# A planner that counts TensorE's switches of tiling, a regular beat for the agents' stage, and a later load of w_out

## The chip, the core and the metric

The kernel runs on one core of a Trainium2 chip. The core has five engines with queues of their own: TensorE (PE; its weight loads are shown as PEld), VectorE (DVE), ScalarE (ACT), GpSimd (POOL) and SyncE (SP), which here issues every DMA. The metric is the device time of one execution in microseconds. The time before is the median of three runs, 1548.81 us (1548.41 to 1549.6).

## The reference

```python
def _attn_ref(q, k, v, agents):            # q, k, v: (4, 12608, 128); agents: (4, 49, 128)
    def sm(a, b): softmax over the last axis of scale * a @ b.T
    agent_v = sm(agents, k) @ v            # (4, 49, 128)
    return sm(q, agents) @ agent_v         # (4, 12608, 128)

def _moe_ref(x, w_in, w_out, g_ln):        # x: (50432, 128), d_ff 1024
    h = x @ w_in
    e = np.exp(h - h.max(-1)); sm = e / (e.sum(-1) + 1e-09)
    solu = h * sm
    ln = (solu - mean(solu)) / sqrt(var(solu) + 1e-06) * g_ln
    return ln @ w_out
```

The second function takes the first one's output, flattened over the four batches. `w_in` and `w_out` arrive as 64-bit floats and are turned into 32-bit floats on the chip.

## The kernel before

**Three stages.** The *agents' stage* (`phase_a`, one call for each batch) goes through the 12608 keys in 13 chunks of 1024 (the last one shorter). For a chunk c it makes the logits of the 49 agents, padded to 64, against the keys (`p1_mm`, line 418, called step M1 here), takes a running maximum (L423, L430) and the exponentials (L444), transposes them on TensorE (L451, step TT), copies them out of PSUM (L457, step ET, on ACT or DVE as the planner likes), and multiplies with v (`p2_mm`, L467, step M2). After the last chunk some small steps (g1 to g7, f0 to f4) make a matrix for the batch, agent_v times w_in, in a high and a low part (`mh`, `ml`). The *q stage* (`phase_b`) works on units of eight tiles of 128 rows of q: logits against the agents (`b0`, L647, step B0), softmax, transposes (L682), and a DMA that lays out the weights pT. The *c stage*, the bulk, goes tile by tile (x = 0 to 395): h in PSUM (`c_h`, L747), maximum (L751), exponential (L761), u (L766), squares (L772), transposes (`c_t`, L779), evictions and a split into high and low parts (L794 to L811), the product with w_out (`c_w`, L827, 24 matmuls for two tiles), and the scaling by the standard deviation.

**Column tiling.** M1, M2 and B0 have stationary operands with 64 columns. Two such matmuls stand side by side in the array, one for PSUM partitions 0 to 63 and one for 64 to 127. Every other step uses all 128 columns. The planner has a mark for that, `kind`: 2 for M1, M2 and B0, 0 for `c_h` and `c_w`, 1 for the rest. A row of adjacent kind-2 steps is called a segment here.

**The order is written out ahead.** Each step is an `op` with an engine, a cost in microseconds, a due time in units of tiles, and what it depends on. `Plan.run` plays the kernel through with these costs: of each engine's candidates it takes those that can start within EPS of the earliest (0.01 us for PE) and of these the one with the lowest due time; of the engines it takes the one that starts first. The instructions come out in that order, and a chain of dependencies (L1029 to L1036) fixes it for each engine except SP, whose order is that of its issues. The costs and due times thus change nothing but the order. SWITCH adds a cost when PE goes from one kind to another: before, nothing into kind 2, and 0.087 or 0.033 us out of it.

**Shared room.** There are four PSUM banks (`px`) for everything but h; an op with `take` waits for a free one, and `free` gives it back: M1 holds its bank until L444 has read it, B0 until L659, the transposes until they are evicted, and one bank holds the sums of `c_w` for four tiles. The chunks of k and v have two buffers each in batches two to four; in batch one, where nothing else runs yet, eight chunks of each fit into buffers of the later stages.

**The head.** For the first batch SP issues (dues near -199) k chunk 0, both halves of w_in, and then k and v chunks in turn, the first q unit after chunk 7, w_out behind v chunk 7 (`VA = 7`), and the second q unit behind v chunk 12 (`VA1 = 12`). The conversions from 64 bits (`pair_f64`, L263) run on DVE, ACT and POOL. That of w_in (`cin`, due -100 + CPR) is needed by step f3 (L531), that of w_out (`cout`) by the first exponential of the c stage, whose buffers it borrows, and what follows it on POOL (L308 to L327), ACT (L331) and DVE (L334) by the first `c_w`.

Of the kernel before, what the change touches and what calls it, by code (L numbers as in the profile page):

```python
# [14 lines left out]
ALU = mybir.AluOpType  # L15
# [10 lines left out]
class Plan:  # L26
# [3 lines left out]
           "AA": 0.0, "AG": 0.17, "GP": 0.25, "GD": 0.1, "GG": 0.1, "GA": 0.2}  # L30
    EPS = {"P": 0.01, "A": 0, "D": 0.07, "G": 2.6, "S": 0.0}

    SWITCH = ((0.0, 0.0, 0.0), (0.0, 0.0, 0.0), (0.087, 0.033, 0.033))

    def __init__(self, banks):
        self.banks = [[0.0, b] for b in banks]
# [25 lines left out]
    def run(self, idle=None):  # L62
        while True:
            best = None
            for e, ops in self.cand.items():
                if not ops:
                    continue
                free = [b[0] for b in self.banks if b[0] is not None]
                first = min(free) if free else None
                at, opts, low = self.at[e], [], None  # L70
                for o in ops:
                    s = max(at, o.ready[e])
                    if o.take:
                        if first is None:
                            continue
                        s = max(s, first)
                    opts.append((s, o))
                    low = s if low is None else min(low, s)
                if low is None:
                    continue  # L80
                s, o = min((z for z in opts if z[0] <= low + self.EPS[e]), key=lambda z: z[1].due)
                if o.shy > 0.0:
                    s, o = min((z for z in opts if z[0] <= s + o.shy), key=lambda z: z[1].due)
                if best is None or s < best[0]:
                    best = (s, e, o)
            if best is None:
                break
            s, e, o = best
            for z in o.eng:
                self.cand[z].remove(o)  # L90
            if o.take:
                can = [b for b in self.banks if b[0] is not None and b[0] <= s]
                bank = max(can, key=lambda b: b[0])
                bank[0], o.bank = None, bank
            if idle is not None and e == "P":
                idle(s - self.at[e])
            o.start, o.by = s, e
            if e == "S":
                hold, size, lag = o.cost
                self.at[e] = s + hold  # L100
                if size:
                    self.dma = max(self.dma, s + 2.0) + size / 0.36
                    o.end = self.dma + 0.3
                else:
                    o.end = s + lag
            else:
                c = o.cost[o.eng.index(e)] if len(o.eng) > 1 else o.cost
                if e == "P":
                    c += self.SWITCH[self.kind][o.kind]
                    self.kind = o.kind  # L110
                o.end = self.at[e] = s + c
            if o.free is not None:
                o.free.bank[0] = o.end + self.LAT[e + "P"]
            if o.fn:
                args = [o.bank[1]] if o.take else []
                if len(o.eng) > 1:
                    args.append(e)
                o.fn(*args)
            for z in o.outs:
                z.left -= 1  # L120
                if not z.left:
                    self.push(z)
# [3 lines left out]
def kernel(  # L126
# [15 lines left out]
    P = 128  # L142
# [4 lines left out]
    NCK = N // (CT * P)  # L147
    CKT = N - NCK * CT * P
    AP2 = 64
    ETE = "AD"  # L150
    CPR = -1.98
    UTB = 4
    DIR = {(1, 0), (1, 1), (3, 1), (5, 1), (7, 1)}
    LGC = 8
    UB = 8
    TD = 2
    WC = 4

    BD0 = 13.69
    BD1 = 8.27  # L160
    BD2 = 9.96
    BD3 = -18.57
    BD4 = 0.41
    BD5 = 5.85
    DH = -3.05
    DMX = -3.31
    DEX = 7.76
    DU_ = 6.48
    DSQ = 21.68
    DT = -0.42  # L170
    DEV = -6.42
    DLD = 1.96
    DSP = 2.68
    DW = 3.31
    DR = 2.33
    DF_ = 5.14
    OUTD = -5.86
    OUTC = -74.58
    VA = 7
    VA1 = 12  # L180
    QA = 8
    WA = 0.5
    VLAG = 0.25
    PTB = 8
    SHY = -2.99
    DHR = -4.59
    DHL = -5.42
    DMXR = 10.02
    DMXL = 15.46
    DEXR = 5.1  # L190
    DEXL = -1.93
    DUR = -10.64
    DUL = -12.84
    DSQR = -10.36
    DSQL = -12.17
    DTR = -6.53
    DTL = -23.81
    DEVR = -0.65
    DEVL = 9.51
    DLDR = -16.59  # L200
    DLDL = 26.96
    DSPR = -6.09
    DSPL = 14.43
    DWR = 0.63
    DWL = -0.21
    RBL = 6.0
    ASTART = -3.67
    AEND = -2.04
    engs = (mybir.EngineType.PE, mybir.EngineType.Activation, mybir.EngineType.DVE, mybir.EngineType.Pool)
    SCALE = 1.0 / math.sqrt(C)  # L210
    INV = 1.0 / DF
# [28 lines left out]
    SL, SR = ALU.logical_shift_left, ALU.logical_shift_right  # L240

    def pair_f64(dst, names):

        ts, tt, stt = nc.vector.tensor_scalar, nc.vector.tensor_tensor, nc.vector.scalar_tensor_tensor
        gt = nc.gpsimd.tensor_tensor
        z = {}

        def tmp():
            for k, tg in (("s", "e"), ("a", "e"), ("e", "u"), ("m", "u")):
                t = epool.tile([P, 2, HW], I32, tag=tg, bufs=2, name=f"c{k}_{names}")  # L250
                for h in range(2):
                    z[k, h] = t[:, h, :]
            for h in range(2):
                z["lo", h], z["hi", h] = (words[names, h][:, :, i] for i in range(2))
                z["r", h], z["d", h], z["di", h] = z["m", h].bitcast(F32), dst[h], dst[h].bitcast(I32)

        def op(k, f, out, cost, **ins):
            def go(h):
                if not z:
                    tmp()  # L260
                kw = {n: (z[v, h] if n != "in1" or f is not gt else z[v, h].bitcast(F32)) if isinstance(v, str) else v
                      for n, v in ins.items()}
                f(out=z[out, h], **kw)  # L263

            return [(k, lambda h=h: go(h), cost) for h in range(2)]

        ops = (
            op("D", ts, "m", 0.34, in0="lo", scalar1=3, scalar2=3, op0=SL, op1=SR)
            + op("A", nc.scalar.mul, "r", 0.52, in_="m", mul=2.0 ** -52)
            + op("D", ts, "e", 0.34, in0="hi", scalar1=1, scalar2=21, op0=SL, op1=SR)  # L270
            + op("D", ts, "e", 0.34, in0="e", scalar1=-896, scalar2=0, op0=ALU.add, op1=ALU.max)
            + op("D", ts, "e", 0.34, in0="e", scalar1=255, scalar2=None, op0=ALU.min)
            + op("D", ts, "s", 0.34, in0="e", scalar1=23, scalar2=None, op0=SL)
            + op("D", ts, "a", 0.34, in0="hi", scalar1=12, scalar2=9, op0=SL, op1=SR)
            + op("G", gt, "r", 1.23, in0="r", in1="s", op=ALU.mult)
            + op("D", tt, "a", 0.6, in0="s", in1="a", op=ALU.bitwise_or)
            + op("D", stt, "a", 0.6, in0="lo", scalar=29, in1="a", op0=SR, op1=ALU.bitwise_or)
            + op("G", gt, "d", 1.23, in0="r", in1="a", op=ALU.add)
            + op("D", stt, "di", 0.6, in0="hi", scalar=-(2 ** 31), in1="di", op0=ALU.bitwise_and, op1=ALU.bitwise_or)
        )  # L280
        return ops[::2], ops[1::2]

# [80 lines left out]
    op = plan.op  # L363
# [9 lines left out]
    def phase_a(b, due, gate):  # L373

        head = b == 0
# [170 lines left out]
        def st(f, *x):  # L546
            return lambda *y: f(*x, *y)
# [2 lines left out]
        sz = lambda c: 0.524 if c < NCK else 0.164  # L550
        fr = lambda c: 1.0 if c < NCK else 0.5
        total = NC * 2.55 + 5.0
        at = lambda z: due[0] + (due[1] - due[0]) * z / total
        bg = op("G", begin, 0.0, at(0), gate)
        K, M1, E1, N1, V, M2, EE, TT, ET, AC = ({} for _ in range(10))

# [12 lines left out]
        for c in range(NC):  # L569
            kop(c)  # L570
            if not head:
                kop(c + 1)
            z = c * 2.55
            M1[c] = op("P", st(p1_mm, c), (0.876 if c < NCK else 0.449) + (0.8 if head and c == 0 else 0.0), at(z),
                       [K[c], M1.get(c - 1), TT.get(c - 2)], take=True, kind=2)
            E1[c] = op("D", st(p1_max, c), 0.6, at(z + 0.3), [M1[c], bg])
            N1[c] = op("D", st(p1_nm, c), 0.07, at(z + 0.4), [E1[c], N1.get(c - 1)])
# [1 line left out]
            if c:  # L579
# [1 line left out]
            TT[c] = op("P", st(p2_t, c), 0.435 * fr(c), at(z + 1), [EE[c], M2.get(c - 2)], take=True)  # L581
            ET[c] = op(ETE, st(p2_et, c), (0.478 * fr(c), 0.6 * fr(c)), at(z + 1.2), [TT[c]], free=TT[c])
            vop(c)
            M2[c] = op("P", st(p2_mm, c), 1.043 if c < NCK else 0.485, at(z + 1.5),
                       [ET[c], V[c], M2.get(c - 1), AC.get(c - 2)], take=True, kind=2)
            AC[c] = op("D", st(p2_ev, c), 0.26, at(z + 1.8), [M2[c], FC.get(c), AC.get(c - 1)], free=M2[c])
        if head:
# [2 lines left out]
        z = NC * 2.55 - 1.5  # L590
# [10 lines left out]
        z = NC * 2.55 + 1.0  # L601
# [32 lines left out]
    def phase_b(k, dues, gate=()):  # L634
# [76 lines left out]
        prev, first = None, None  # L711
        for j0, j1 in chunks:
            f = (lambda px, j0=j0, j1=j1: b0(j0, j1, px)) if prev is None else (lambda j0=j0, j1=j1: b0(j0, j1))
            o = op("P", f, 0.155 * (j1 - j0), dues[0] + 0.1 * j0,
                   [BQ[k], prev, B0.get(k - 1)] + [B4.get((k - 2, q)) for q in range(2)] + list(gate), take=prev is None, kind=2, shy=shy)
            first = first or o
            prev = o
# [224 lines left out]
    def at(x, d, r, l):  # L942
        return x + d + (r * (1.0 - x / 12.0) if x < 12 else l if x >= (B - 1) * TB else 0.0)
# [134 lines left out]
```

## Time and profile before

| what | before |
|---|---|
| median of three runs | 1548.81 us (1548.41 to 1549.6) |
| profiled execution, its own time | 1548.65 us |
| span of its instructions | 1546.9 us |
| TensorE clock granted | 1.0 throughout |
| DVE, ACT, POOL busy | 89%, 92%, 81% of the span |

A timeline row gives the start, the time until the end of the last instruction in the row, the engine, the line, and what is written and read. A matmul's busy time includes its way through the array, so neighbours overlap: what a step takes from TensorE is read from start to start. "x16" is a count of instructions merged into a row. A value in square brackets is idle time before it, with what ended it.

### The profile page before, as it was taken

The numbers are of one execution on the slowest core, as the hardware profiler recorded it, in microseconds if no ns is written. First come the engines' busy times: TensorE is split into PE (matmuls) and PEld (weight loads), VectorE is DVE, ScalarE is ACT, GpSimd is POOL, SyncE is SP. The second block draws the span as 40 slices with busy tenths as digits, with TensorE's granted clock in tenths as the row PEclk, the third lists the DMA queues.
The fourth block names the chain that finished last, engine by engine and source line by source line (L and its number), as shares of the span: only waits on it lengthen the run. The fifth ranks groups of instructions, "written<-read, shape, count | busy, mean of one in ns | idle before, by whom it ended". The sixth has DMA issues, their size and how long they took to land.

```text
span 1546.9 us, 35512 instructions
## 1 busy us (share of the span) xinstructions
PE 1526.4 (99%) x12628; PEld 1356.1 (88%) x12628; DVE 1372.4 (89%) x2214; ACT 1421.6 (92%) x2738; POOL 1252.9 (81%) x1613
## 2 busy tenths in 40 slices
PE   8899999999999999999999999999999999999998
PEld 4588898998889889898898889898889999999998
DVE  6988998888898889898898889889899999999997
ACT  3599999999899999999999999999999999999997
POOL 1478878787888887888878887887788899898987
PEclk9999999999999999999999999999999999999999
DMA  9533333324233333332333334433222232222221
GB/s 370 186 104 100 107 98 115 117 69 127 81 97 118 103 110 117 112 102 83 106 98 101 111 97 117 116 100 105 78 76 75 68 90 76 71 82 70 68 62 46
DMA packets 114721, 159.65 MB, mean 103 GB/s; under 512 B 16240, under 2 KB 71152, under 8 KB 114544
## 3 DMA queue, kind: packets, MB, share of 16 engines
q1 hardware_dynamic: 114544, 157.39, 34.0%
q8 instruction: 100, 1.64, 0.4%
q14 instruction: 77, 0.63, 0.1%
HBM read 105.36 MB, written 26.02 MB: 85 GB/s over the span
## 4 chain that ended last, share of the span: by engine, by line
PE 95%; DVE 3%; ACT 1%; DMA 1%; issue 0%; SPq 0%; DVEq 0%; ACTq 0%
PE px L827 36%; PE ph L747 24%; PE px L779 23%; PE px L647 3%; PE px L467 3%; PE px L418 3%; PE px L451 1%; PE px L682 1%; PE px L531 0%; DMA pT<-pn 0%; DVE mxp L423 0%; DVE nm L751 0%; DMA kh<-in_kT_dram 0%; DVE ca_in L263 0%; DVE uL L803 0%
## 5 line engine op out<-in xcount | busy, mean ns | idle before, releaser
L811 POOL TENSOR_TENSOR uL<-uT,uH 128x1024 fp32r<-128x1024 f32 (+1 forms) x344 | 661.5, 1923 | 27.6
L751 DVE TENSOR_REDUCE nm<-ph 128x1 f32<-128x1024 f32 x396 | 481.3, 1217 | 50.5 <-PE ph L747 47.7
L766 DVE SCALAR_TENSOR_TENSOR u<-ph,e 128x1024 f32<-128x1024 f32 x396 | 479.0, 1217 | 34.6 <-ACT e L761 24.4
L772 ACT ACTIVATE sq<-u,su 128x1024 bf16<-128x1024 f32 x396 | 460.5, 1163 | 24.8 <-DVE u L766 20.4
L761 ACT ACTIVATE e<-ph,nm 128x1024 f32<-128x1024 f32 x396 | 445.9, 1128 | 31.9 <-DVE nm L751 30.7
L827 PE MATMUL px<-uL,wH 128*128 128x256 f32 x1584 | 466.9, 295 | 0.2 <-POOL uL L811 0.2
L827 PE MATMUL px<-uH,wH 128*128 128x256 f32 x1584 | 450.6, 284 | 1.8 <-DVE uL L803 1.8
L827 PE MATMUL px<-uH,wL 128*128 128x256 f32 x1584 | 448.1, 283 | 0.0
L779 PE MATMUL px<-ident,u 128*128 128x128 f32 x3168 | 425.5, 274 | 2.7 <-DVE uL L803 1.4
L779 PEld LDWEIGHTS px<-ident,u 128*128 128x128 f32 x3168 | 356.7, 141 | 55.2 <-issue 20.7
L807 POOL TENSOR_SCALAR uH<-uT 128x1024 fp32r<-128x1024 f32 (+1 forms) x344 | 298.3, 867 | 98.4 <-ACT uT L798 98.0
L747 PE MATMUL ph<-mh,pT 128*128 128x512 f32 x792 | 329.7, 416 | 1.6 <-DMA pT<-pn 1.3
L827 PEld LDWEIGHTS px<-uH,wH 128*128 128x128 f32 x1584 | 299.0, 189 | 16.9 <-issue 3.5
L747 PE MATMUL ph<-ml,pT 128*128 128x512 f32 x792 | 312.3, 394 | 0.0
L798 ACT COPY uT<-px 128x512 f32<-128x512 f32 x541 | 299.2, 589 | 11.9 <-PE px L779 3.0
L827 PEld LDWEIGHTS px<-uH,wL 128*128 128x128 f32 x1584 | 299.1, 189 | 8.6 <-issue 0.7
L827 PEld LDWEIGHTS px<-uL,wH 128*128 128x128 f32 x1584 | 298.9, 189 | 8.5 <-issue 4.6
L803 DVE TENSOR_TENSOR uL<-px,uH 128x512 fp32r<-128x512 f32 x251 | 168.8, 685 | 47.5 <-ACT uH L794 45.8
L747 PEld LDWEIGHTS ph<-mh,pT 128*128 128x128 f32 x792 | 149.3, 188 | 20.3 <-issue 3.4
L747 PEld LDWEIGHTS ph<-ml,pT 128*128 128x128 f32 x792 | 149.9, 189 | 17.7 <-issue 0.5
L794 ACT CAST uH<-px 128x512 fp32r<-128x512 f32 x251 | 143.7, 592 | 1.2 <-PE px L779 0.9
L846 POOL TENSOR_TENSOR y<-x,nhalf 128x4 f32<-128x4 f32 x99 | 100.1, 1011 | 7.7
(118 smaller groups left out, 1337.6 us busy)
## 6 DMA issues: line engine op xcount, KB each, us to landing
pT<-pn SPq DMA_DIRECT2D x392, 64.0 KB
rB<-dr SPq DMA_DIRECT2D x98, 256.0 KB
qt<-in_qT_dram SPq DMA_DIRECT2D x48, 512.0 KB
out_dram<-ob SPq DMA_DIRECT2D x95, 256.0 KB
kt<-in_kT_dram SPq DMA_DIRECT2D x36, 512.0 KB
vt<-in_v_dram SPq DMA_DIRECT2D x36, 512.0 KB
dr<-yr SPq DMA_DIRECT2D x392, 0.5 KB
kh<-in_kT_dram SPq DMA_DIRECT2D x12, 512.0 KB
```

The costliest lines, as they stand in the source:

```text
L747: nc.tensor.matmul(ph[:, sl], lhs, bmats[b]["mh" if m == 0 else "ml"][:, sl], start=(m == 0), stop=(m == 1))
L751: nc.vector.tensor_reduce(out=nms[x], in_=phs[x], op=ALU.max, axis=AX.X, negate=True)
L761: nc.scalar.activation(out=es[x], in_=phs[x], func=AF.Exp, bias=nms.pop(x), accum_out=st[G]["S"][:, j : j + 1])
L766: nc.vector.scalar_tensor_tensor(out=u, in0=phs[x], scalar=INV, in1=es[x], op0=ALU.mult, op1=ALU.mult, accum_out=su)
L772: nc.scalar.activation(out=sq, in_=u, func=AF.Square, bias=su, scale=-float(DF), accum_out=st[G]["Q"][:, j : j + 1])
L779: nc.tensor.transpose(pt[:, kf * P : (kf + 1) * P], us[x][0][:, k0 * P : (k0 + 1) * P], ident)
L794: nc.scalar.copy(out=uH, in_=pt)
L798: nc.scalar.copy(out=rr[x][:, hf * 4 : hf * 4 + 4, :], in_=pt)
L803: nc.vector.tensor_tensor(out=uL, in0=pt, in1=uH.bitcast(F32), op=ALU.subtract)
L807: nc.gpsimd.tensor_scalar(out=uH, in0=rr[x][:, k0:k1, :], scalar1=1.0, scalar2=0.0, op0=ALU.mult, op1=ALU.add)
L811: nc.gpsimd.tensor_tensor(out=uL, in0=rr[x][:, k0:k1, :], in1=uH.bitcast(F32), op=ALU.subtract)
L827: nc.tensor.matmul(po, wt[:, kf, :], ut[:, kf, :], start=(q == 0), stop=(q == WM - 1))
```

## The change

The planner gets a cost for going into kind 2 and a higher one for leaving it. While PE is in kind 2, any kind-2 op that can start within HOLD (0.17 us) of the earliest candidate is taken ahead of the others, whatever its due time. The planner's costs of M1, M2, B0 and of three conversion ops are set anew.

In batches two to four the agents' stage no longer spreads its steps over the time from ASTART to AEND, but goes at a fixed beat: a chunk each UB * ASP = 6.8 tiles (a q unit has 8). M2 of chunk c is due 6.8 * 2.36 / 2.55 = 6.3 tiles after its M1, so just ahead of the M1 of chunk c + 1 at 6.8; before it was due 1.5 / 2.55 of a beat of 7.0 tiles after its M1, which is 4.1.

In the head w_in is issued ahead of k chunk 0 (WA), v chunks come three k chunks later (VLAG), w_out moves behind k and v of chunk 12 (VA), and so stands ahead of the second q unit, which was there already. The first q unit's load has a later due time (QA). The conversion of w_in is due after the steps of the first batch's agents' stage instead of before them (CPR). The due times of the other steps have new values.

```diff
-    SWITCH = ((0.0, 0.0, 0.0), (0.0, 0.0, 0.0), (0.087, 0.033, 0.033))
+    SWITCH = ((0.0, 0.0, 0.12), (0.0, 0.0, 0.12), (0.18, 0.14, 0.0))
+
+    HOLD = 0.17
...
-                s, o = min((z for z in opts if z[0] <= low + self.EPS[e]), key=lambda z: z[1].due)
+                near = [z for z in opts if z[0] <= low + self.EPS[e]]
+                if e == "P" and self.kind == 2:
+                    near = [z for z in opts if z[0] <= low + self.HOLD and z[1].kind == 2] or near
+                s, o = min(near, key=lambda z: z[1].due)
...
-    CPR = -1.98
+    CPR = 1.32
...
-    BD0 = 13.69
-    BD1 = 8.27
-    BD2 = 9.96
-    BD3 = -18.57
-    BD4 = 0.41
-    BD5 = 5.85
-    DH = -3.05
-    DMX = -3.31
-    DEX = 7.76
-    DU_ = 6.48
-    DSQ = 21.68
+    BD0 = 14.77
+    BD1 = 12.82
+    BD2 = 19.94
+    BD3 = -16.84
+    BD4 = -1.74
+    BD5 = 4.61
+    DH = -3.24
+    DMX = 8.3
+    DEX = 0.49
+    DU_ = -2.17
+    DSQ = 18.46
...
-    OUTD = -5.86
+    OUTD = -13.17
...
-    VA = 7
+    VA = 12
...
-    QA = 8
-    WA = 0.5
-    VLAG = 0.25
+    QA = 22.85
+    WA = -5.59
+    VLAG = 0.61
...
-    ASTART = -3.67
-    AEND = -2.04
+    ASP = 0.85
+    MZ = 2.36
+    ASTART = -3.92
+    AEND = -6.25
...
-        at = lambda z: due[0] + (due[1] - due[0]) * z / total
+        at = lambda z: due[0] + (due[1] - due[0]) * z / total if head else due[0] + UB * ASP * z / 2.55
...
-            M1[c] = op("P", st(p1_mm, c), (0.876 if c < NCK else 0.449) + (0.8 if head and c == 0 else 0.0), at(z),
+            M1[c] = op("P", st(p1_mm, c), (0.95 if c < NCK else 0.51) + (0.8 if head and c == 0 else 0.0), at(z),
...
-            M2[c] = op("P", st(p2_mm, c), 1.043 if c < NCK else 0.485, at(z + 1.5),
+            M2[c] = op("P", st(p2_mm, c), 0.96 if c < NCK else 0.45, at(z + MZ) if not head else at(z + 1.5),
...
-            o = op("P", f, 0.155 * (j1 - j0), dues[0] + 0.1 * j0,
+            o = op("P", f, 0.128 * (j1 - j0), dues[0] + 0.1 * j0,
```

Left out are new values of the remaining due times and three costs of conversion ops (0.6 to 0.9).

More of the change, by code (lines that the diff above doesn't have):

```diff
@@ L157 @@
     WC = 4
-    BD0 = 13.69
-    BD1 = 8.27
-    BD2 = 9.96
-    BD3 = -18.57
-    BD4 = 0.41
-    BD5 = 5.85
-    DH = -3.05
-    DMX = -3.31
-    DEX = 7.76
-    DU_ = 6.48
-    DSQ = 21.68
-    DT = -0.42
[L171 to L176, printed above, removed]
-    OUTD = -5.86
+    BD0 = 14.77
[9 more added lines that the diff above has]
+    DSQ = 18.46
+    DT = -0.42
+    DEV = -7.32
+    DLD = 2.24
+    DSP = -1.16
+    DW = 3.3
+    DR = 15.18
+    DF_ = 5.63
+    OUTD = -13.17
     OUTC = -74.58
-    VA = 7
+    VA = 12
     VA1 = 12
-    QA = 8
-    WA = 0.5
-    VLAG = 0.25
+    QA = 22.85
+    WA = -5.59
+    VLAG = 0.61
     PTB = 8
[L185 to L192, printed above, removed]
+    SHY = -0.0
+    DHR = -4.39
+    DHL = -5.43
+    DMXR = -5.18
+    DMXL = 10.25
+    DEXR = 23.76
+    DEXL = -1.81
+    DUR = -10.37
     DUL = -12.84
-    DSQR = -10.36
+    DSQR = -10.73
     DSQL = -12.17
     DTR = -6.53
-    DTL = -23.81
-    DEVR = -0.65
+    DTL = -23.89
+    DEVR = -12.92
     DEVL = 9.51
@@ L202 @@
     DSPR = -6.09
-    DSPL = 14.43
-    DWR = 0.63
+    DSPL = 14.3
+    DWR = 2.02
     DWL = -0.21
     RBL = 6.0
-    ASTART = -3.67
-    AEND = -2.04
+    ASP = 0.85
+    MZ = 2.36
+    ASTART = -3.92
+    AEND = -6.25
     engs = (mybir.EngineType.PE, mybir.EngineType.Activation, mybir.EngineType.DVE, mybir.EngineType.Pool)
@@ L275, in pair_f64 @@
             + op("G", gt, "r", 1.23, in0="r", in1="s", op=ALU.mult)
-            + op("D", tt, "a", 0.6, in0="s", in1="a", op=ALU.bitwise_or)
-            + op("D", stt, "a", 0.6, in0="lo", scalar=29, in1="a", op0=SR, op1=ALU.bitwise_or)
+            + op("D", tt, "a", 0.9, in0="s", in1="a", op=ALU.bitwise_or)
+            + op("D", stt, "a", 0.9, in0="lo", scalar=29, in1="a", op0=SR, op1=ALU.bitwise_or)
             + op("G", gt, "d", 1.23, in0="r", in1="a", op=ALU.add)
-            + op("D", stt, "di", 0.6, in0="hi", scalar=-(2 ** 31), in1="di", op0=ALU.bitwise_and, op1=ALU.bitwise_or)
+            + op("D", stt, "di", 0.9, in0="hi", scalar=-(2 ** 31), in1="di", op0=ALU.bitwise_and, op1=ALU.bitwise_or)
         )
```

## The prediction

> **What bounds the kernel now.** I read the page first: the busy shares, then the chain that ended last.
>
> ```profile
> span 1546.9 us, 35512 instructions
> ...
> PE 1526.4 (99%) x12628; PEld 1356.1 (88%) x12628; DVE 1372.4 (89%) x2214; ACT 1421.6 (92%) x2738; POOL 1252.9 (81%) x1613
> ...
> PE 95%; DVE 3%; ACT 1%; DMA 1%; issue 0%; SPq 0%; DVEq 0%; ACTq 0%
> ```
>
> TensorE is busy for all but 20.5 us, and 95% of the chain is its work. To see where the rest lies I ask for windows: the head, a stretch of batch two with all three stages, and batch four, which has no agents' stage beside it. Columns are length, then busy time (and instructions) of PE, PEld, DVE, ACT, POOL, then clock, DMA share and GB/s. Under them stand the two longest of PE's waits after 75 us.
>
> ```profile
> 0.00:75.00 75.00, 62.27 (x575) 39.37 (x575) 57.76 (x124) 31.95 (x76) 26.32 (x36) 1.00 0.78 282
> ...
> 420.00:770.00 350.00, 350.00 (x2912) 312.89 (x2911) 312.02 (x498) 331.70 (x639) 286.55 (x367) 1.00 0.36 106
> ...
> 1150.00:1500.00 350.00, 350.00 (x2896) 322.60 (x2895) 325.04 (x505) 343.26 (x649) 312.95 (x407) 1.00 0.26 74
> ```
> ```profile
> PE px L779 <- DVE uL L803: 1.4, 1, 1.4
> PE ph L747 <- DMA pT<-pn: 1.3, 1, 1.3
> ```
>
> In both later windows PE has no idle time at all, at full clock; ACT comes next with 331.7 and 343.3 us of 350. So from about 75 us on the time is the sum of what PE's instructions take, start to start, and a gain must come out of that sum or out of the head. No matmul is added or removed, so the sum can only change where it depends on the order.
>
> **Does the order cost PE anything?** I look at the timeline of PE around steps of kind 2. First an M2 alone, between matmuls of `c_w`:
>
> ```profile
> 92.08 0.28 PE L827 MATMUL px<-uH,wH 128*128 128x256 f32 x1
> 92.19 0.28 PE L827 MATMUL px<-uL,wH 128*128 128x256 f32 x1
> 92.39 1.09 PE L467 MATMUL px<-vt,eT 128*64 128x128 f32 x16
> 93.42 0.39 PE L827 MATMUL px<-uH,wL 128*128 128x256 f32 x1
> ```
>
> Within `c_w` starts are 0.11 us apart; the M2 starts 0.20 after the last one. Going in costs 0.09. The M2 holds PE for 1.03 (92.39 to 93.42). Now an M1 alone (its row is also the first kind-2 step after 75 us), and then an M1 and an M2 that happen to stand together in the head:
>
> ```profile
> 80.48 1.08 PE L418 MATMUL px<-kt,ag_sb 128*64 128x512 f32 x4
> 81.49 0.39 PE L827 MATMUL px<-uL,wH 128*128 128x256 f32 x1
> ```
> ```profile
> 26.28 1.08 PE L418 MATMUL px<-kh,ag_sb 128*64 128x512 f32 x4
> 27.19 1.04 PE L467 MATMUL px<-vh,eT 128*64 128x128 f32 x16
> 28.16 0.66 PE L451 MATMUL px<-ident,ek 128*128 128x128 f32 x4
> ```
>
> The M1 takes 1.01 alone and 0.91 ahead of another kind-2 step: leaving costs 0.10. The M2 takes 0.97 behind the M1 instead of 1.03. The join saved 0.09 + 0.10 + 0.06 = **0.25 us**. The other end of what I find is a B0 joined with an M1, against a B0 alone (two rows of the chain in order of time):
>
> ```profile
> 455.04 1.14 PE L647 MATMUL px<-ag_sb,qt 128*64 128x49 f32 x32
> 456.07 1.08 PE L418 MATMUL px<-kt,ag_sb 128*64 128x512 f32 x4
> 457.08 0.66 PE L779 MATMUL px<-ident,u 128*128 128x128 f32 x4
> ```
> ```profile
> 428.62 1.07 PE px L647 x32
> 429.69 1.14 PE px L779 x8
> ```
>
> Joined the B0 takes 1.03, alone 1.07, and the M1 still 1.01; with the entry of 0.09 that is **0.13 us**. I take the middle, 0.19 us for a join, and keep 0.13 and 0.25 for the range.
>
> [...]
>
> **How many joins.** The counts after 75 us, from the views of the three lines, and the last kind-2 step of the program:
>
> ```profile
> L418 PE MATMUL px<-kt,ag_sb x156: 222/593/643, 80.5 to 1134.2; 128*64 128x512 f32 x144, 128*64 128x256 f32 x6, 128*64 128x64 f32 x6
> ```
> ```profile
> L467 PE MATMUL px<-vt,eT x594: 269/273/324, 89.0 to 1148.9; 128*64 128x128 f32 x195, 64*64 64x128 f32 x3
> ```
> ```profile
> L647 PE MATMUL px<-ag_sb,qt x1456: 222/222/258, 140.9 to 1486.4; 128*64 128x49 f32 x182
> ```
> ```profile
> 1486.04 0.56 PE L647 MATMUL px<-ag_sb,qt 128*64 128x49 f32 x12
> ```
>
> By four, sixteen (six in a tail) and thirty-two (twelve in a tail) these are 39 M1, 39 M2 and 48 B0: 126 steps. From the row at 80.48 to that at 1486.04 they stand in 122 segments, since only four touch. 13 segments are B0s after the last agents' stage, with nothing to join; 109 are left, 36.3 in each of the three stages.
>
> After the change: an M2 becomes due 6.3 tiles after its M1 and the next M1 0.5 later; when the M2 runs, HOLD takes that M1 at once, if its keys are there (their load is due eight tiles ahead) and a bank is free. Thirteen chunks give 14 segments: the first M1, twelve pairs, the last M2. A B0 comes each 8 tiles. It draws an M2 along, and with it the next M1, if that M2 is ready. When is it? In the trace of before one chunk reads:
>
> ```profile
> 100.26 1.08 PE L418 MATMUL px<-kt,ag_sb 128*64 128x512 f32 x4
> ...
> 105.07 0.72 ACT L444 ACTIVATE ek<-px,nmp 128x512 f32<-128x512 f32 x1
> ...
> 120.53 0.62 ACT L457 COPY eT<-px 128x512 f32<-128x512 f32 x1
> ...
> 123.31 0.88 PE L467 MATMUL px<-vt,eT 128*64 128x128 f32 x12
> ```
>
> From the groups of ACT in the window 420 to 770, one exponential for each tile:
>
> ```profile
> L761 ACT ACTIVATE e<-ph,nm 128x1024 f32<-128x1024 f32 x92 | 103.2, 1124 | 7.8 <-DVE nm L751 7.5
> ```
>
> A tile takes some 3.8 us (350 us over 92), the exponential of the chunk is done 1.4 tiles after the M1, and the transposes and copies follow when due: at 2.7 and 3.2 tiles of the new beat. So an M2 is ready in about the second half of each beat, and of the 11 B0s of a stage I let half be joined. That leaves 14 + 5.5 alone + 2 B0s outside the stage = 21.5 segments, 14.8 fewer for a stage, 44.5 in all. **44.5 x 0.19 = 8.5 us less.** Ends: 25 joins at 0.13 (3.3 us) if pairs often miss each other, 61 at 0.25 (15.3 us) if every B0 is joined too.
>
> What hides nothing here: the saved time is PE's own, and in the windows PE is the only engine without idle time. What would be late next is ACT; a fall of 0.8% takes its share in 420 to 770 from 94.8% to 95.5%, and batch four runs at 98.1% with PE still full.
>
> **The head.** Its rows:
>
> ```profile
> 1.77 0.90 SPq L289 DMA_DIRECT2D wd_in<-in_w_in_dram  x2
> ...
> 5.65 1.12 PE L418 MATMUL px<-kh,ag_sb 128*64 128x512 f32 x2 [1.44 <-DMA kh<-in_kT_dram]
> ```
> ```profile
> 21.09 1.66 SPq L295 DMA_DIRECT2D wd_out<-in_w_out_dram  x2
> ...
> 39.29 1.03 DVE L263 TENSOR_SCALAR cm_out<-wd_out 128x512 int32<-128x512 int32 x2
> ...
> 57.74 0.94 DVE L263 SCALAR_TENSOR_TENSOR w<-wd_out,w 128x512 int32<-128x512 int32 x1
> ...
> 65.66 1.11 ACT L761 ACTIVATE e<-ph,nm 128x1024 f32<-128x1024 f32 x1 [0.26 <-DVE nm L751]
> ```
> ```profile
> 74.44 0.36 PE L827 MATMUL px<-uH,wH 128*128 128x256 f32 x1 [1.77 <-DVE uL L803]
> ```
>
> w_in ahead of k chunk 0 moves two issues of 0.45 us and 1 MB past it: the first M1 (5.65) comes 0.9 us later by the issues alone, up to some 3 by the bytes. w_out behind chunk 12 moves two issues (1.66 us on SP, whose queue is full there) past five chunks of k and five of v: these come about 2 us sooner, and w_out's words that much behind them, about when DVE began on them before (39.29). DVE is the tight engine of the head (57.8 us busy of 75). Before, conversions of w_in stood ahead of the first chunks; now chunks go first and the conversion fills gaps. But DVE's work up to the first exponential is the same. With the first batch's steps ahead, the conversion of w_out, 19.4 us from 39.29 to 58.68, can hardly end sooner; the first exponential (65.66) may come a few us sooner, the first `c_w` (74.44), which waits for what POOL makes of w_out, hardly. I put the head at **1 us less**, between 5 less (DVE loses its idle time) and 4 more (w_out's conversion starts late and takes as long).
>
> The new due times among DVE's and ACT's ops move no work between engines; PE's waits after 75 us come to under 4 us, so at most that is to be gained, and I put it at nothing. The tail is the same.
>
> **Sum.** Profiled time 1548.65 - 8.5 - 1 = 1539.2 us; the median stands 0.16 above that execution, so **1539.3 us**.
>
> **The rivals.** *Slower: banks.* A segment of three steps takes three of the four banks, and an M1 keeps its one until the exponential (100.26 to 105.8 above). Meanwhile the transposes (L779), two a tile, have one or none, and PE runs out of `c_w` matmuls. If that costs one transposed half's turn-round now and then, say 0.35 us in each of some 42 segments of the three stages, it is 14.7 us: 1539.3 + 14.7 = 1554. It decides from 8.5 / 42 = 0.2 us a segment. For it: PSUM is shared by all three stages, and HOLD looks at no due time. Against it: behind the joined pair at 455.04, PE goes on without a gap; and the planner counts banks. [...] No row of before shows it binding. Chance 0.13.
>
> *The order changes little.* HOLD needs the M2 to be ready and the M1's bank free within 0.17 us. In before, the copy L457 ends only 2 us ahead of its M2; if the planner keeps putting it off, pairs split. 25 joins or fewer: 3.3 us, 1545.5, on the edge of no change. Chance 0.17.
>
> *The head gives back.* w_in first and w_out last cost the full 4 us: 1544.3. Chance 0.10.
>
> *More than counted.* Every B0 joined at the upper price, or 5 us out of the head: 1530 to 1533. Chance 0.05.
>
> **The numbers.** The forecast has 0.55 (by itself 1533 to 1545). About 0.2%, 3.1 us, can be told from no change: faster means under 1545.7. Faster: 0.55 + 0.10 + 0.05 + 0.06 of the second rival = 0.76; same 0.11; slower 0.13. The range takes in the ends of the two unknown sums, 1529, and above it no change and the lower half of the slower rival, 1552.
>
> **What would show it.** Kind-2 segments after 75 us fall from 122 to some 77; M1, M2 and B0 rows stand next to each other; PE stays at 350 of 350 in mid-kernel windows; the first `c_w` is near 74 us. I am wrong if PE shows waits for evictions behind segments (banks), if segments stay above 95, or if the first `c_w` comes past 78.

## The result and the profile after

| what | before | after |
|---|---|---|
| median, measured side by side (7 runs each) | 1549.60 us (1548.41 to 1551.73) | 1560.93 us (1558.52 to 1568.27) |
| ratio to before, 95% interval | | 1.0081 [1.0061, 1.0102] |
| profiled execution | 1548.65 us | 1558.91 us |
| TensorE clock granted, mean | 1.0 | 0.995 |
| kind-2 segments after 75 us | 122 | 51 |

The change makes the kernel 0.8% slower, 11.3 us. The forecast was 1539.3, faster, and the time lies outside its range of 1529 to 1552. Lines of after's code stand 7 below those of before: `c_h` is now L754, the transposes L786, `c_w` L834, M1 L425, M2 L474, B0 L654.

First the head of the page of after, then its windows, with columns as in the prediction (length, busy time and instructions of PE, PEld, DVE, ACT, POOL, clock, DMA share, GB/s):

```profile
span 1556.9 us, 35392 instructions
...
PE 1512.3 (97%) x12581; PEld 1352.9 (87%) x12581; DVE 1381.1 (89%) x2226; ACT 1418.0 (91%) x2726; POOL 1255.7 (81%) x1613
...
PE 74%; DVE 9%; ACT 6%; DMA 5%; issue 3%; POOL 1%; SPq 1%; DVEq 0%; ACTq 0%; POOLq 0%
```
```profile
0.00:75.00 75.00, 57.38 (x499) 36.61 (x500) 57.68 (x129) 33.09 (x77) 26.31 (x37) 0.94 0.75 273
...
420.00:770.00 350.00, 346.65 (x2891) 313.04 (x2890) 312.68 (x500) 328.65 (x633) 287.46 (x364) 1.00 0.34 104
...
1150.00:1500.00 350.00, 346.90 (x2886) 319.65 (x2885) 323.84 (x500) 340.86 (x645) 314.23 (x398) 1.00 0.25 73
```

PE's busy time did fall, from 1526.4 to 1512.3 us. But the chain of the end, 95% PE before, is now 74% PE, and DVE, ACT and DMA stand in it. PE has lost its 350 of 350: some 3 us are idle in each window, in batch two and in batch four alike. What ended that idle time is in the view of waits after 75 us (engine, line waited for, total, times, longest):

```profile
DVE ob L899 <- DMA rB<-dr: 16.8, 13, 3.6
...
PE ph L754 <- DMA pT<-pn: 7.7, 8, 2.0
...
PE px L786 <- DVE logits L666: 3.1, 1, 3.1
...
PE px L786 <- DVE u L773: 2.4, 2, 1.5
PE px L786 <- DVE ob L899: 2.0, 3, 1.0
```

The first of these lines is new and the second has grown: before had no wait of DVE for the DMA of `rB`, and one of 1.3 us for `pT`. Both are DMAs in the middle of a chain of computation (256 KB in one issue, and four issues of 64 KB). `rB` brings the row of reciprocals, turned round through DRAM (`yr` to `dr` to `rB`), to all partitions, where DVE multiplies the output by it (`ob`). `pT` brings the packed weights of half a q unit (four tiles) to `c_h`.

**How a late `rB` stops PE** is seen in one stretch of the timeline of after, SP's part first, then DVE's, then PE's:

```profile
175.65 1.81 SPq L875 DMA_DIRECT2D dr<-yr  x4
...
177.89 3.52 SPq L713 DMA_DIRECT2D pT<-pn  x4
...
181.57 0.48 SPq L876 DMA_DIRECT2D rB<-dr  x1
```
```profile
182.47 0.34 DVE L483 SCALAR_TENSOR_TENSOR av<-av,fc,px 128x128 f32<-128x128 f32 x1
186.39 0.69 DVE L899 TENSOR_TENSOR ob<-px,rB 128x512 f32<-128x512 f32 x1 [3.57 <-DMA rB<-dr]
187.00 0.56 DVE L660 TENSOR_REDUCE mx<-px 128x8 f32<-128x392 f32 x1
187.59 0.57 DVE L666 TENSOR_TENSOR logits<-px,mx 128x392 f32<-128x392 f32 x1
```
```profile
181.78 1.05 PE L654 MATMUL px<-ag_sb,qt 128*64 128x49 f32 x30
182.87 1.08 PE L425 MATMUL px<-kt,ag_sb 128*64 128x512 f32 x4
...
184.45 0.40 PE L754 MATMUL ph<-mh,pT 128*128 128x512 f32 x1
184.68 0.40 PE L754 MATMUL ph<-ml,pT 128*128 128x512 f32 x1
188.21 1.09 PE L786 MATMUL px<-ident,u 128*128 128x128 f32 x8 [3.13 <-DVE logits L666]
189.06 0.36 PE L834 MATMUL px<-uL,wH 128*128 128x256 f32 x1
...
189.85 0.63 PE L754 MATMUL ph<-mh,pT 128*128 128x512 f32 x1
190.28 0.63 PE L754 MATMUL ph<-ml,pT 128*128 128x512 f32 x1
```

SP issues the four parts of `dr` at 175.65, then four of `pT`, which take it 3.52 us, then `rB` at 181.57. DVE has come to `ob` at 182.8 and stands there for 3.57 us. Behind `ob` in its queue is the evicting of the B0 that PE did at 181.78 (`mx` and `logits`), which does not need `rB`. So B0's bank stays taken, the M1 beside it holds another, the sums that `ob` itself reads hold a third, and the transposes cannot start until `logits` is done: PE is idle for 3.13 us. For a few us it is also slow: `c_h` goes at 0.43 us a matmul (189.85 to 190.28) instead of 0.23 (184.45 to 184.68). In before the same group of four tiles had 9.9 us between `rB`'s issue and its `ob`, and no wait:

```profile
166.25 0.34 SPq L869 DMA_DIRECT2D rB<-dr  x1
...
176.16 0.68 DVE L892 TENSOR_TENSOR ob<-px,rB 128x512 f32<-128x512 f32 x1
```

**The whole of it as a ledger.** I add up PE's matmuls after 75 us, from the start of one to the start of the next, with idle time apart. An interval that leads into a segment belongs to a full-width matmul; what it has over the mean of the others is the segment's entry, and is put with kind 2. Before and after differ a little in what falls behind 75 us, so they are compared by the matmul:

| PE after 75 us | before | after |
|---|---|---|
| idle | 3.6 us | 22.3 us |
| kind-2 matmuls with entry and exit | 138.1 us, 2206: 62.6 ns each | 124.2 us, 2238: 55.5 ns each |
| full-width matmuls | 1325.5 us, 9846: 134.6 ns each | 1329.9 us, 9843: 135.1 ns each |

The change did what it says: 7.1 ns less for each of 2238 kind-2 matmuls is 15.9 us, 0.22 us for each of the 71 joins. But 18.7 us of idle time came in their place, the full-width matmuls cost 4.9 us more (0.5 ns x 9843), and 32 kind-2 matmuls more, with 3 full-width ones fewer, fall behind 75 us: 1.6 us of work that the head left over. 18.7 - 15.9 + 4.9 + 1.6 = 9.3 of the 10.3 us between the two profiled executions. Why the full-width matmuls cost more was not settled; a part of it, an estimated 1.4 us, is the lower clock behind the wait above (0.66 over 4 us, last section).

### The profile page after: what moved, and what is told of

Read it like the earlier page. It is cut to its first block, busy times and chain, and to the rows that moved or that the text cites. A ratio compares the mean times of both kernels' runs of the same rounds, so it can differ in the third digit from the quotient of the medians.

```text
span 1556.9 us, 35392 instructions
## 1 busy us (share of the span) xinstructions
PE 1512.3 (97%) x12581; PEld 1352.9 (87%) x12581; DVE 1381.1 (89%) x2226; ACT 1418.0 (91%) x2726; POOL 1255.7 (81%) x1613
## 4 chain that ended last, share of the span: by engine, by line
PE 74%; DVE 9%; ACT 6%; DMA 5%; issue 3%; POOL 1%; SPq 1%; DVEq 0%; ACTq 0%; POOLq 0%
PE px L834 28%; PE ph L754 19%; PE px L786 18%; DVE u L773 3%; PE px L474 2%; DMA rB<-dr 2%; ACT sq L779 2%; PE px L425 2%; ACT e L768 2%; PE px L654 2%; DVE nm L758 2%; DMA pT<-pn 1%; ACT uT L805 1%; PE px L458 1%; PE px L689 1%
## 5 line engine op out<-in xcount | busy, mean ns | idle before, releaser
L834 PE MATMUL px<-uL,wH 128*128 128x256 f32 x1584 | 466.6, 295 | 0.0
L786 PE MATMUL px<-ident,u 128*128 128x128 f32 x3168 | 429.3, 275 | 19.8 <-DVE u L773 13.3
L834 PE MATMUL px<-uH,wL 128*128 128x256 f32 x1584 | 448.3, 283 | 0.0
L834 PE MATMUL px<-uH,wH 128*128 128x256 f32 x1584 | 448.0, 283 | 0.3 <-DVE nmp L435 0.3
L786 PEld LDWEIGHTS px<-ident,u 128*128 128x128 f32 x3168 | 361.0, 141 | 61.7 <-DVE u L773 14.2
L754 PE MATMUL ph<-mh,pT 128*128 128x512 f32 x792 | 332.7, 420 | 9.7 <-DMA pT<-pn 7.7
L754 PE MATMUL ph<-ml,pT 128*128 128x512 f32 x792 | 313.8, 396 | 0.2
L805 ACT COPY uT<-px 128x512 f32<-128x512 f32 x541 | 301.0, 590 | 12.8 <-PE px L786 6.1
L834 PEld LDWEIGHTS px<-uH,wH 128*128 128x128 f32 x1584 | 299.3, 189 | 10.7 <-issue 1.5
L834 PEld LDWEIGHTS px<-uH,wL 128*128 128x128 f32 x1584 | 299.4, 189 | 6.7
L834 PEld LDWEIGHTS px<-uL,wH 128*128 128x128 f32 x1584 | 299.2, 189 | 3.5 <-issue 0.4
L754 PEld LDWEIGHTS ph<-mh,pT 128*128 128x128 f32 x792 | 150.0, 189 | 39.0 <-issue 13.5
L754 PEld LDWEIGHTS ph<-ml,pT 128*128 128x128 f32 x792 | 150.6, 190 | 17.1 <-DVE ml L550 0.9
```

Source lines behind the costliest of these rows:

```text
L754: nc.tensor.matmul(ph[:, sl], lhs, bmats[b]["mh" if m == 0 else "ml"][:, sl], start=(m == 0), stop=(m == 1))
L786: nc.tensor.transpose(pt[:, kf * P : (kf + 1) * P], us[x][0][:, k0 * P : (k0 + 1) * P], ident)
L805: nc.scalar.copy(out=rr[x][:, hf * 4 : hf * 4 + 4, :], in_=pt)
L834: nc.tensor.matmul(po, wt[:, kf, :], ut[:, kf, :], start=(q == 0), stop=(q == WM - 1))
```

## The experiments

The theory: the new due times took the lead, the time from a DMA's issue to its first reader, away from `rB` and `pT`. `DR` (2.33 to 15.18) puts the reciprocals later, `BD4` and `BD5` (0.41 to -1.74 and 5.85 to 4.61) shift the packing of a q unit. From the timelines, the median time from `rB`'s issue to the first `ob` that reads it (98 cases) fell from 13.5 to 5.6 us, and from the end of the last issue of a `pT` to its first `c_h` (96 cases, without the first four) from 8.0 to 4.6 us. The rivals: banks, held by joined segments; and the head.

### Without the reader of `rB`, in after and in before

The output is multiplied by a constant tile of ones in place of the reciprocals; the DMAs still run.

```diff
-                                in1=st[G]["rB"][:, j0:j1], op=ALU.mult)
+                                in1=fixed[:, j0:j1], op=ALU.mult)
```

In after:

> The kernel after, but c_fin multiplies by a fixed tile of ones instead of rB: the scaling by the standard deviation is left out, the DMAs to rB still run, and nothing waits for them. The order on every engine is unchanged. Theory 1 (late DMAs: the new due times leave rB and pT too little time): the 16.8 us in which DVE waits for rB go, of PE's 22.3 us of idle time after 75 us some 10 go, and the time falls by 8 to 12 us, from 1560.9 to about 1550. Theory 2 (banks: joined steps hold PSUM banks and transposes wait): PE's waits stay, within 3 us of after. Theory 3 (the head costs it): within 3 us of after.

Measured: 1548.15 us (1545.6 to 1553.64), ratio to before 0.9992 [0.9979, 1.0005]. That is 12.8 us less than after, a little more than the 8 to 12 expected, from one operand. The same edit in before is the control:

> The control: the same edit in the kernel before, which shows 1.8 us of DVE waiting for rB in all. All theories: within 1.5 us of before (1549.6).

Measured: 1547.49 us, ratio 0.9983 [0.9974, 0.9993]; 2.0 us less than before, a little more than expected. (The 1.8 us in the expectation are misread: in before no `ob` waits for the DMA of `rB`; 1.8 us is an `ob` that waited for a matmul, L747.) So nearly 11 us of the 12.8 are the change's own. What is left in after without `rB`:

```profile
PE ph L756 <- DMA pT<-pn: 8.7, 7, 2.8
...
PE px L788 <- DVE u L775: 4.3, 1, 4.3
```

PE's waits for `pT` are as long as ever. They are the next to take out.

### Without the readers of `rB` and of `pT`

`c_h` reads a fixed tile as well, in place of the packed weights. This frees it from all that comes before `pT`, the packing too, and not from the DMA alone.

```diff
-        lhs = pTs[b, g][:, j * P : (j + 1) * P]
+        lhs = fixed_pt[:, j * P : (j + 1) * P]
```

> The kernel after with the edit of the first run, and c_h takes a fixed tile instead of pT: h no longer depends on the attention, the DMAs to pT still run, and nothing waits for them. Theory 1: PE's 7.7 us of waiting for pT go as well, idle time of PE after 75 us falls from 22.3 us to under 6, and the time to about 1543, 6 us under before, which is what the joins should give. Theory 2: more than 15 us of idle time stay, with evictions and L666 as what ends them. Theory 3: the time stays over 1553, and the loss is there at the first matmul of c_w.

Measured: 1534.95 us (1533.18 to 1536.84), ratio to before 0.9902 [0.9886, 0.9919]. Another 13.2 us, more than expected. The window from 75 us on, in after and then with both readers gone:

```profile
75.00:1500.00 1425.00, 1402.66 (x11687) 1267.69 (x11687) 1277.85 (x2029) 1337.38 (x2562) 1186.42 (x1513) 1.00 0.31 95
```
```profile
75.00:1500.00 1425.00, 1420.44 (x11866) 1287.95 (x11865) 1299.43 (x2063) 1358.64 (x2606) 1207.91 (x1542) 1.00 0.31 96
```

In the same 1425 us PE does 179 more matmuls, and its idle time falls from 22.3 to 4.6. By the ledger (same work after 75 us in both) 17.8 us of the 26.0 are PE's idle time and 6.6 the quicker matmuls between. No wait of PE for an eviction of a transposed half is left among the long ones (the longest is 0.6 us); the segments, 51 after 75 us, are the same. So banks taken by joined segments can stop PE for no more than these 4.6 us by themselves. The control again:

> The control of the third run: both edits (c_fin takes a fixed tile instead of rB, c_h a fixed tile instead of pT, so the scaling is left out and h does not depend on the attention) in the kernel before. Before shows 1.3 us of PE waiting for pT, and without rB it took 1547.5. If lateness is what the change brought (theory 1): 1546 to 1548, so that 12 us or so lie between this and the third run (1534.95), the worth of the joins. If before hides as much behind these two DMAs: under 1540.

Measured: 1544.53 us, ratio 0.9971 [0.996, 0.9982]. Before had 4.7 us of this kind too, again more than expected: by the ledger 2.8 us of it are PE's idle time (3.6 to 0.8 after 75 us) and 0.8 quicker matmuls; where the rest lies was not settled. So of the 26.0 us in after, **21.3 are the change's own**; and with these two readers gone on both sides, the change is worth 1544.53 - 1534.95 = **9.6 us less**, head included. The forecast was 9.5 less, but that the two agree is luck: by the ledger the joins alone bring 15.8 us between these two kernels (7.0 ns for each of 2238 kind-2 matmuls), far more than the 8.5 forecast, and more idle time of PE (3.8 us) and other work give a part of it back.

### What the joins are worth: HOLD off

After without both readers, with the rule alone taken out (the due times, the switch costs and the beat stay):

```diff
-    HOLD = 0.17
+    HOLD = -1.0
```

> The third run's kernel (after, without the waits for rB and pT, with what that leaves out) with HOLD off: kind-2 steps are no longer drawn together and stand in 138 segments of the program instead of 68, all costs, due times and the head as in after. If a join is worth 0.19 us: 1535 + 70 x 0.19 = 1548. If the joins were worth nothing and the due times made the third run fast: within 2 us of 1535.

Measured: 1554.37 us (1553.82 to 1555.76), ratio to before 1.0035 [1.0022, 1.0048], 19.4 us over the kernel with the rule. It has 138 segments in the whole program instead of 68: 19.4 / 70 = 0.28 us for each. That is above the 0.13 to 0.25 that I read from rows, though the other due times were chosen with the rule in place, and may fit less well without it. The ledger takes this apart: the kind-2 matmuls with entry and exit go from 55.6 to 62.4 ns each, 15.4 us or 0.22 for each of 71 segments after 75 us, as between before and after. Another 7.5 us lie in the full-width matmuls (mainly 134.4 to 135.1 ns each), and 3.3 us of idle time go. A run below gives the other end.

### The head of before

After with the head's order as it was before:

```diff
-    CPR = 1.32
+    CPR = -1.98
...
-    OUTD = -13.17
+    OUTD = -5.86
...
-    VA = 12
+    VA = 7
...
-    QA = 22.85
-    WA = -5.59
-    VLAG = 0.61
+    QA = 8
+    WA = 0.5
+    VLAG = 0.25
```

> The kernel after with the head of before (w_in behind k chunk 0, w_out behind v chunk 7, conversion of w_in first; WA, VLAG, QA, VA, CPR, OUTD). Theory 3: 6 us or more faster than after. Theories 1 and 2: the body keeps its waits, within 4 us of after; rB and pT waits of 15 us or more stay (DVE for rB, PE for pT).

Measured: 1556.91 us (1551.12 to 1559.97), ratio 1.0043 [1.003, 1.0056], 4.0 us less than after. The waits for `rB` stay:

```profile
DVE ob L899 <- DMA rB<-dr: 20.4, 17, 2.6
```

The head costs some time, and is not the main cause. The median leads are as short in this run (5.5 us for `rB`, 4.6 for `pT`) as in after, and so they are in the run without HOLD above (5.6 and 4.1). So neither the head nor the rule took the lead away; the due times, the beat and the planner's costs are left, and were not taken apart.

### Lead put back by the planner

If lead is what is missing, the planner should be able to give it, with nothing left out. It had been told that `rB` is there 6.0 us after the first issue of `dr` (`RBL`), and that a `pT` takes 0.24 us of SP and is there some 2.7 us after its issue. The traces show, for `rB`, 3.4 us from the first `dr` issue to its own (mean) and 3.1 to 6.4 us more until an `ob` starts that waits for it (13 in after), together 6.5 to 9.8; for `pT`, four issues of some 0.6 us each, 2.4 of SP. Two kernels with more of that in the planner, the head of before, the rule, switch costs as the rows had them (0.09 in, 0.10 out), and the due times searched anew for the least planned time. First the fuller figures:

```diff
-    RBL = 6.0
+    RBL = 10.0
...
-            pT_op[groups[g]] = op("S", lambda q=q: b8(q), (0.24, 0.13 if k else 0, 2.5), dues[5] + 2.5 * q + 0.6,
+            pT_op[groups[g]] = op("S", lambda q=q: b8(q), (2.4,0,5.5), dues[5] + 2.5 * q + 0.6,
```

> Nothing is left out. The rule of the change (SWITCH at the measured 0.09 in and 0.10 out, HOLD 0.17) and the head of before; the planner is told that rB lands 10 us after it is first issued instead of 6, and that pT holds SP for 2.4 us and lands after 5.5 instead of 0.24 and 2.7; due times found anew by the planner's own end under these latencies (DSQ 18.5 to 3.0, BD5 4.6 to 9.1, DF_ 5.6 to 7.1 and others). 75 segments. Theory 1: DVE waits for rB under 4 us in all and PE for pT under 3, time 1535 to 1542, faster than before. Theory 2 (banks): PE waits for evictions come in their place, not under 1547.

Measured: 1534.87 us (1533.31 to 1535.45), ratio 0.9906 [0.9891, 0.992], the fast end of what was expected. PE's two longest waits after 75 us are now

```profile
PE ph L754 <- DVE u L773: 1.8, 4, 1.1
PE px L834 <- ACT uT L805: 1.1, 1, 1.1
```

and none of PE's is for a DMA. Then figures about half way, `RBL` 8.0 and (1.0, 0, 4.5) for `pT`:

> The same with latencies between: rB after 8 us, pT holding SP for 1.0 us and landing after 4.5; due times found anew, 71 segments; the planner's own end is 3 us earlier than that of the other. Theory 1: some lateness is left (rB 4 to 10 us on DVE), time between the other and after, 1538 to 1550. Theory 2: like the other, or better by the 3 us that the planner sees.

Measured: **1533.11 us** (1531.53 to 1535.18), ratio **0.9894** [0.9876, 0.9911], as the second theory had it: of the lateness that the first expected, little is left. It is the fastest kernel here: 16 us below before, 28 below after (7 of them by the head, see below), with the full computation. Its wait for `rB`, and the window from 75 us:

```profile
DVE ob L899 <- DMA rB<-dr: 2.4, 3, 1.4
```
```profile
75.00:1500.00 1425.00, 1420.73 (x11830) 1288.80 (x11829) 1290.36 (x2057) 1362.63 (x2616) 1208.51 (x1545) 1.00 0.31 96
```

16.8 us in 13 waits have become 2.4 in 3. The median lead of `rB` is only 6.7 us (5.6 in after), but its short end has moved: a tenth of the leads lie under 4.7 us instead of 3.5, a quarter under 5.7 instead of 4.1. For `pT` the shortest lead is 14.3 us. With 51 segments after 75 us, as many as in after, PE is idle for 4.3 us there.

### The latencies without the rule, and the best kernel with the new head

The last kernel's latencies and head, HOLD off, the beat of before, and due times searched anew for that:

> The control of t2: the same latencies told to the planner (rB 8 us, pT 1.0 and 4.5), the same head (of before) and the same measured SWITCH, but HOLD off and the agents' stage spread as in before; due times found anew with the same effort. 135 segments; the planner's own end is 10.6 us later than for t2. If t2's gain comes from the joins: 1543 to 1549, as before without its two waits (1544.5). If a new search of due times alone brought it: 1533 to 1538.

Measured: 1543.14 us (1542.12 to 1544.79), ratio 0.9957 [0.9943, 0.9972], with 135 segments in the whole program. That is 6.3 us less than before, by the fuller latencies and the new search together; lead alone is not shown by it, since `rB`'s median lead is 13.1 us here and was 13.5 in before. The rule with the beat adds 10.0 us more for 64 joins: 0.16 us each, where the due times fit both sides. With the 0.28 above, whole kernels give 0.16 to 0.28 us for a join. The ledger gives 0.23 for this pair too (61.9 to 55.3 ns for each of 2206 kind-2 matmuls, 63 segments after 75 us); PE's idle time and the full-width matmuls take 5.7 us of it back. Both kernels' due times come out of a search, so a us or two between them may be chance.

The best kernel with the head of after (the six values of the diff above turned round):

> t2 with the head of the change (w_in ahead of k chunk 0, w_out and second q unit behind all k and v; WA, VLAG, QA, VA, CPR, OUTD), all else the same. If the new head costs what the run with the old one suggested: 3 to 7 us slower than t2, 1536 to 1540 (the planner sees 6). If the head is neutral, as the times of tile 24 in after suggested: within 2 us of 1533.

Measured: 1540.28 us (1539.1 to 1540.64), ratio 0.9936 [0.992, 0.9953]; 7.2 us slower than with the head of before, the slow end of what was expected.

## Why the prediction was wrong

**What bounds the kernel: right for before, and the weak point.** PE was the bound, and saved PE time was there to be had. But that PE does not wait held only while each transfer had lead enough, and the prediction looked at waits, not at how near they were.

**The price and number of joins: right mechanism, sizes off.** I had 0.19 us for a join (0.13 to 0.25); whole kernels give 0.16 to 0.28, the ledger 0.22 or 0.23 in three pairs. I counted 44.5 joins, with half of the B0s joined; it was 71. Two stretches of PE's timeline in after show the typical segments:

```profile
515.28 1.09 PE L474 MATMUL px<-vt,eT 128*64 128x128 f32 x16
516.20 1.03 PE L425 MATMUL px<-kt,ag_sb 128*64 128x512 f32 x4
517.06 1.09 PE L654 MATMUL px<-ag_sb,qt 128*64 128x49 f32 x32
518.08 0.50 PE L754 MATMUL ph<-mh,pT 128*128 128x512 f32 x1
...
646.00 1.09 PE L474 MATMUL px<-vt,eT 128*64 128x128 f32 x16
646.93 1.09 PE L654 MATMUL px<-ag_sb,qt 128*64 128x49 f32 x32
647.85 1.04 PE L425 MATMUL px<-kt,ag_sb 128*64 128x512 f32 x4
648.82 0.50 PE L754 MATMUL ph<-mh,pT 128*128 128x512 f32 x1
```

M2, M1 and B0 stand in one segment, in either order. HOLD looks at no due time, so a B0 that could start is drawn along whenever a pair runs. Ahead of another kind-2 step each takes 0.86 to 0.93 us of PE here; alone, in the prediction's rows, an M1 took 1.01, an M2 1.03 and a B0 1.07. The upper bound of my sum (61 joins at 0.25, 15.3 us) was nearer than the value that I took.

**"The new due times among DVE's and ACT's ops move no work between engines; PE's waits after 75 us come to under 4 us, so at most that is to be gained, and I put it at nothing." This step failed.** It asked how much there was to gain, and never how much to lose. Due times move no work between engines, but they do move the start of each DMA's chain against its reader (here the median lead of `rB` went from 13.5 to 5.6 us). The prediction weighed neither `DR` nor the two DMAs (of `pT` it showed a single wait of 1.3 us), though the timeline of before had both leads. The term that it put at nothing measured 21.3 us more, two and a half times what the joins were forecast to bring:

| | us |
|---|---|
| change with both readers gone on both sides (head included) | -9.6 |
| lead of `rB` and `pT`, the change's own (26.0 - 4.7) | +21.3 |
| sum | +11.7 |
| measured in all | +11.3 |

(All rows are differences of the same few times, so the sum has to come out and proves nothing; it stands 0.4 off since the before of its runs is not the same set as that of the first table.)

**The head: forecast 1 less, measured as a loss.** I let 5 less to 4 more stand; the runs give 4.0 more in after and 7.2 more in the best kernel. PE's waits in the head of after, and its first `c_w`:

```profile
8.90 3.36 PE L425 MATMUL px<-kh,ag_sb 128*64 128x512 f32 x8 [4.69 <-DMA kh<-in_kT_dram]
...
63.17 1.97 PE L786 MATMUL px<-ident,u 128*128 128x128 f32 x8 [6.45 <-DVE u L773]
...
73.17 1.93 PE L786 MATMUL px<-ident,u 128*128 128x128 f32 x8 [4.42 <-DVE u L773]
...
81.46 0.38 PE L834 MATMUL px<-uH,wH 128*128 128x256 f32 x1 [0.32 <-DVE nmp L435]
```

The first M1 comes at 8.90 instead of 5.65: w_in's megabyte ahead of the first keys costs the 3 us that I had as the upper figure. The first `c_w` comes at 81.46, past the 78 that I had named as a sign of being wrong: w_out is converted later, and PE waits twice for the first tiles (the first exponential does come sooner, at 58.57 instead of 65.66). Two things the prediction did not see: its "No matmul is added or removed" leaves out that in the head the planner fills gaps that it foresees on PE with matmuls on ones (`ph<-ones`, 92 in before, 45 in after; all others are the same in number), and the granted clock of the first 75 us is 0.94 in after instead of 1.00. What each costs was not tried. In after itself most of that seems made up by tile 24 (its exponential is 0.7 us ahead of before's, the `c_w` of that tile 1.5 behind), and the ledger finds 1.6 us of work left over, while the run with the old head gives 4.0. How much of after's time is the head's stays open between these; the 7.2 hold for the best kernel.

**The rivals.** *Banks*, the slower one, had the right place and the wrong cause, so that its 1554 lies nearest to the measured time is luck: the transposes did wait for a bank, but because DVE, which had to empty it, stood at `rB` (3.57 us in the stretch above). With the DMAs' readers gone, or with lead in the plan, about as many joined segments leave PE idle for 3 to 5 us after 75 us (3.2 in the kernel with the fuller figures, 4.3 in the best, 4.6 without the readers). *The order changes little* falls with 51 segments. *The head gives back* came true on top. *More than counted* held for the joins; its sum, 1530 to 1533, was met only by the best kernel, which has the head of before, and not by after.

**What would have shown it ahead of the result.** The leads of `rB` and `pT` in before: medians of 13.5 and 8.0 us, a tenth of `pT`'s under 4.6, and the issues of both behind others on SP. Of the 6.0 us that the planner gave `rB` from the first issue of `dr`, 3.4 had gone by in before when `rB` was issued, on average, so that a plan could leave it 2.6 us to land. (In after, the readers that waited started 3.1 to 6.4 us behind `rB`'s issue and 0.9 to 4.1 us behind the end of `pT`'s last.) A change that makes `DR` later and reorders the packing has a loss to be bounded there, 194 times, and it could not be put at nothing.

## What to carry to other kernels

When due times or the order of an already full kernel change, list each DMA that stands inside a chain of computation and compare its lead, from issue to first reader, with how long it takes at worst: a wait that the profile doesn't show may be near. In a planner, a DMA's cost is its time on the issuing queue (a `pT` held SP for 2.4 us here), what stands ahead of it there, and a landing time with room for its spread (3.1 to 6.4 us from the issue of `rB` to the start of an `ob` that waited for it); the plan of after, with the short landing, took 20.7 us more on the chip than one searched with 2 us more of it and the same head (1560.93 against 1540.28). Here DVE, standing 3.57 us at `ob`, held up the op queued behind it that frees a bank, and PE stood for 3.13 us, so an idle bound engine is to be followed back past the engine that it names.

## What was not expected of the hardware

PE's clock in after falls for a few us around or after an idle stretch, also a short one. Windows around the 6.45 us of the head and the 3.13 us at 185.1:

```profile
60.00:63.00 3.00, 0.00 (x0) 0.00 (x0) 3.00 (x4) 0.91 (x1) 2.92 (x3) 0.50 0.89 285
63.00:67.00 4.00, 3.83 (x17) 3.43 (x18) 2.94 (x8) 2.00 (x5) 2.87 (x5) 0.57 0.13 50
...
188.00:192.00 4.00, 3.79 (x19) 3.30 (x20) 3.01 (x8) 3.38 (x7) 1.04 (x1) 0.66 0.65 198
```

The granted clock is 0.50 in the last 3 us of the long stretch, 0.57 in the 4 us behind it, and 0.66 on average in the 4 us after the short one, so a wait of 3 us can cost more than its length (here an estimated 1.4 us more, 0.34 of those 4 us). The clock went to half 2.9 us into the long stretch, but around the short one only 4.2 us after it began, when PE was at work again (1.00 over 185.08 to 189.30, 0.50 over 189.31 to 192.71). A stretch of 2.82 us in the run without the reader of `rB` was followed by a lower clock too (0.57 over the 4 us from 246), while one of 3.03 us in the head of the latencies without the rule left the clock at 1.00. So in these runs the length of one idle stretch does not decide it alone. That kernels with such waits also spread wider (after 1558.5 to 1568.3, the best kernel 1531.5 to 1535.2) would fit, and of after's seven executions the four longest have the lowest mean clock (0.987 to 0.992, the others 0.995 and 0.996); it was not tried by itself.

The same broadcast (`rB`) released its reader between 3.1 and 6.4 us after its issue, by the 13 `ob` rows of after that waited for it. What it stood behind in the slow cases was not settled.
